# Attention and two MLPs on one core: where the second MLP's weight slabs and next inputs are requested, and an empty step in the weight preparation

## The chip, the cores and the metric

One core of one Trainium2 chip runs the whole program in one launch. The metric is the device time of that core in microseconds; the kernel before took 999.39 us (median of three runs, 997.2 to 1000.39).

## The reference, cut to what matters

```
attn  = softmax(causal(q k^T / 8 + min(-(cum_i - cum_j), 0))) v     B=4, H=8, S=576, D=64
x     = attn as 2304 tokens x 512
h     = x @ w_in1 (512x2048);  g = max(h,0) + alpha*min(h,0);  x = g @ w_out1 (2048x512)
h     = x @ w_in2 (512x2048);  g = max(h,0)^2;                  out = g @ w_out2 (2048x512)
```

All inputs are float32, and cum is the running sum of max(s, 0).

## The kernel before

Each float32 operand of a matmul is split into a high and a low part, and each product is three matmuls (high by high, high by low, low by high). TensorE (PE) therefore has three times the plain work, and the rest of the program is built around keeping it fed.

The program has three parts. **Attention** comes first. **The first MLP** walks 48 steps: three passes of 768 tokens (two halves of 384), and 16 blocks of 128 hidden units in each. One step has 24 matmuls of the first product (line 551, tiles ph) and 24 of the second (line 672, tiles po); VectorE (DVE) applies the activation to ph (lines 570, 571), ScalarE (ACT) and DVE split the result into gs (lines 573, 574), and both split the weights of the next step (lines 526, 527: wi_hi and wi_lo, wo_hi and wo_lo). At the change of a pass the finished sums are copied out of PSUM (evac, lines 260 and 262) and the next inputs are split (xs, lines 537 and 538).

**The second MLP** multiplies 2x2 blocks with seven products in place of eight (the Winograd form of Strassen's scheme), again in three passes. A pass has a first stage (stage1: eight blocks q, seven products of six matmuls in each, line 790, weights w1h) and a second (Stage2.run: 28 items of 18 matmuls, line 917, weights w2s and inputs th). The first stage's weights come from DRAM in groups (w1_group: tile w1f, four buffers, split by ACT and DVE into w1h, five buffers; four groups to a block q, 32 to a pass). The second stage's come in slabs of 1 MB (w2_slab: tile w2s, four buffers, 14 to a pass). The inputs of the next pass come with load_x (four requests, tile xl). All of these are requests on one queue, SyncE's (SP), which works in order.

These weights don't exist in the inputs: they are sums of blocks of w_in2 and w_out2, and the program makes them **during the first MLP**. A list todo says at which of the 48 steps each piece of that work is emitted. For w_in2 a block q is prep_conv twice (two ACT copies at lines 114 and 115, two DVE operations at 116 and 117, an addition on GpSimd (POOL) at 120, which together rebuild one weight tile from raw_w into the tile wc) and prep_sums (four POOL additions in wc and a store of wc to w1D, line 156). There is one buffer of wc, so the next block's first write into it, ACT's at line 115, has to wait until the store has read it. For w_out2 a block is two prep_conv, prep_sums and two prep_split (whl, lines 164 and 165, then a store to w2D). The pieces are spread evenly over steps 13 to 44 by their position in the list.

The order on each engine is not the order of the source. The compiler's planner reorders instructions by its own estimate of when each is ready, within what the data allow; a block `with tc.issue_after(x)` holds what it contains behind instruction x in that order. In the kernel before nothing holds the slabs and the next inputs of the second MLP, which is why they stand on SP's queue where the planner thought that they could go.

Words used below: a **group** is one w1f request with its split into w1h; a **slab** is one w2s request.

Of the kernel before, what the change touches and what calls it, by code (L numbers as in the profile page):

```python
# [19 lines left out]
def attention_then_two_mlps(  # L20
# [13 lines left out]
    nc = tc.nc  # L34
# [12 lines left out]
    NPASS = B * S // (2 * HT)  # L47
    NQ = NF // 2
# [84 lines left out]
    SLOT = {1: 0, 6: 1, 5: 2, 2: 3, 7: 4, 4: 5, 3: 6}  # L133
    w1D = dr.tile([NQ, P, 7, 256], F32, name="w1D")
# [423 lines left out]
    def ins_of(x):  # L558
        return x.ins if hasattr(x, "ins") else x
# [47 lines left out]
    for g in range(len(units) + LAG + PVLAG):  # L607
        live = g < len(units)
        if live:
            n, i = units[g]  # L610
            i = g % 5
# [75 lines left out]
    sub = []  # L687
    for which in range(2):
        for q_ in range(NQ):
            loads += [(1, q_ + z * NQ, which) for z in range(2)]  # L690
            sub += [(prep_conv, (which, q_, 0)), (prep_conv, (which, q_, 1)), (prep_sums, (which, q_))]
            if which:
                sub += [(prep_split, (q_, 0)), (prep_split, (q_, 1))]
    first_prep, last_prep = NF - NPRE, (NPASS - 1) * NF + NF - NPRE - 1
    todo += [(first_prep + (last_prep - first_prep) * z / len(sub), *t) for z, t in enumerate(sub)]
    for _ in range(2):
# [7 lines left out]
    def split2(dst, src):  # L704

        a = nc.scalar.copy(dst[:, 0], src)  # L706
        v = nc.vector.tensor_sub(dst[:, 1], src, dst[:, 0].bitcast(F32))  # L707
        return ins_of(a), ins_of(v)

    def load_x(p):  # L710
        xl = xa01.tile([P, NKB, W], F32, name="xl", tag="x0")
        for i, j in ((0, 0), (0, 1), (1, 1), (1, 0)):
            r, c = slice(2 * i, 2 * i + 2), slice(j * HT, (j + 1) * HT)
            nc.sync.dma_start(xl[:, r, c], xD[p][:, r, c])
        xl_now[0] = xl
# [5 lines left out]
    def x_steps():  # L721


        xl = xl_now[0]
        x_parts()
        b11, b12, b21, b22 = (xl[:, 2 * i : 2 * i + 2, j * HT : (j + 1) * HT] for i in range(2) for j in range(2))

        def put(i, src):
            split2(xc[i], src)

        def diff(dst, a, b):
            nc.vector.tensor_sub(dst, a, b)

        return [
            lambda: put(1, b11), lambda: diff(b12, b12, b11), lambda: put(5, b12),
            lambda: diff(b12, b22, b12), lambda: put(6, b12), lambda: diff(b11, b12, b11),
            lambda: put(2, b21), lambda: put(7, b11), lambda: diff(b21, b21, b12),
            lambda: put(4, b21), lambda: put(3, b22),
        ]

    GROUPS = ((0, 2), (2, 2), (4, 2), (6, 1))

    def w1_group(q, g):
        s0, k = GROUPS[g]
        wt = pools["w1"].tile([P, 512], F32, name="w1f", tag="w1f", bufs=4)
        nc.sync.dma_start(wt[:, : k * 256].rearrange("p (k c) -> p k c", k=k), w1D[q][:, s0 : s0 + k, :])
        hl = pools["w1"].tile([P, 2, 512], F32R, name="w1h", tag="w1h", bufs=5)
        split2(hl[:, :, : k * 256], wt[:, : k * 256])
        return hl

    def w2_slab(s, hq):
        t = pools["m2"].tile([P, 2, 4, 256], F32R, name="w2s", tag="w2s", bufs=4)
        nc.sync.dma_start(t.bitcast(F32), w2D[s, hq])
        return t
# [9 lines left out]
    class Stream:  # L764
# [5 lines left out]
        def fetch(self, n):  # L770
            while self.next < min(len(W1_ORDER), n):
                self.ready[W1_ORDER[self.next]] = w1_group(*W1_ORDER[self.next])
                self.next += 1
# [76 lines left out]
    class Stage2:  # L850


        def __init__(self, p):
            self.p = p
            self.items = [(i, q) for i in ORDER2 for q in range(NQ // 2)]
            self.th, self.slab, self.done = {}, {}, 0

        def prepare(self, n):

            while self.done < min(n, len(self.items)):  # L860
                i, q = self.items[self.done]
                self.done += 1
                if q % 2 == 0:
                    self.slab[i, q // 2] = w2_slab(SLOT[i], q // 2)
                gq = g_t[q]
                if i == 6:
                    nc.vector.tensor_sub(gq[:, :, 1], gq[:, :, 3], gq[:, :, 1])
                elif i == 7:
                    nc.vector.tensor_sub(gq[:, :, 0], gq[:, :, 1], gq[:, :, 0])
                elif i == 4:  # L870
                    nc.vector.tensor_sub(gq[:, :, 2], gq[:, :, 2], gq[:, :, 1])
                th = pools["m2"].tile([P, 2, 2, HT], F32R, name="th", tag="th", bufs=3)
                self.last = split2(th, gq[:, :, PLACE[i]])
                self.th[i, q] = th
# [130 lines left out]
    for p in range(NPASS):  # L1005
        s2 = Stage2(p)

        def early(left):
            if left == 0:
                s2.prepare(AHEAD)  # L1010
            if left == NQ // 2 and p + 1 < NPASS:
                load_x(p + 1)

        stage1(stream if p == 0 else Stream(), early)
        steps2 = x_steps() if p + 1 < NPASS else []

        def fill(n):
            if n >= 3 and n % 2 == 1 and steps2:
                with tc.issue_after(s2.last[0]), tc.issue_after(s2.last[1]):
                    steps2.pop(0)()  # L1020

        s2.run(fill)
        assert not steps2
# [30 lines left out]
```

## Time and profile before

| | us |
|---|---|
| median of three runs | 999.39 |
| lowest and highest run | 997.2, 1000.39 |
| profiled execution: span from first to last instruction | 998.7 |
| PE busy in it | 970.2 (97%) |
| DVE, ACT, POOL busy | 806.6 (81%), 561.9 (56%), 401.5 (40%) |
| granted TensorE clock, mean | 0.990 |

The page gives the profiled execution by its span alone, 998.7 us; it lies 0.7 us under the median of the runs. PE is the engine whose idle time counts; the busy share of the others says only how close they are to becoming the ones that PE waits for. The trace also gives the granted clock of each stretch: 1.00 is 2.4 GHz, 0.50 is 1.2 GHz, and values between are mixtures over the stretch.

### The profile page before, as it was taken

What the parts mean: (1) busy time and instruction counts of PE and PEld (TensorE: products, weight loads), DVE (VectorE), ACT (ScalarE), POOL (GpSimd) and SP (SyncE); (2) the same over time, 40 slices, a digit from 0 to 9 for tenths busy, and PEclk for the clock granted to TensorE, in tenths of its full rate; (3) what the DMA queues carried; (4) which work ended last, traced back from release to release, by engine and by line L of the source; (5) the groups of instructions that cost most, each with busy time, mean ns of one, the idle gap of its engine ahead of it and who ended that gap; (6) DMA issues with size and microseconds to landing.
All of it is one profiled execution on the core that took longest, in us unless ns stands there. A gap on an engine that the chain in (4) does not pass through costs nothing.

```text
span 998.7 us, 18060 instructions
## 1 busy us (share of the span) xinstructions
PE 970.2 (97%) x6440; PEld 899.7 (90%) x6440; DVE 806.6 (81%) x1552; ACT 561.9 (56%) x1120; POOL 401.5 (40%) x478
## 2 busy tenths in 40 slices
PE   6999999999999999999999999899999999999998
PEld 6677778788999989989999999899999999999998
DVE  8899889869888897878887768578985889668774
ACT  7788889964555544434554434456453664446442
POOL 7788777634333445553342220335002440034400
PEclk9899999999999999999999999989999999999999
DMA  7766454304444334436454341944687446754274
GB/s 175 172 155 162 121 123 119 73 19 142 127 127 127 133 126 159 158 127 201 150 170 134 127 142 40 365 128 148 219 274 268 127 155 236 266 179 130 97 250 139
DMA packets 105050, 157.06 MB, mean 157 GB/s; under 512 B 31584, under 2 KB 80224, under 8 KB 99584
## 3 DMA queue, kind: packets, MB, share of 16 engines
q1 hardware_dynamic: 104960, 155.91, 49.7%
q8 instruction: 51, 0.84, 0.3%
q14 instruction: 39, 0.32, 0.1%
HBM read 117.00 MB, written 29.88 MB: 147 GB/s over the span
## 4 chain that ended last, share of the span: by engine, by line
PE 68%; DVE 14%; DMA 6%; POOL 4%; ACT 4%; issue 4%; SPq 0%; DVEq 0%; POOLq 0%; ACTq 0%
PE acc L917 15%; PE ph L551 11%; PE po L672 10%; PE b L790 4%; PE a L790 4%; PE c L790 4%; PE ps_tr L443 3%; PE ps_xb L493 3%; PE d L790 2%; PE ps_xa L482 2%; DMA w1D<-wc 2%; PE ps_sc L357 2%; DVE gg L570 2%; PE ps_sc L358 2%; POOL wc L120 2%
## 5 line engine op out<-in xcount | busy, mean ns | idle before, releaser
L551 PE MATMUL ph<-xs,wi_hi 128*128 128x384 f32 x768 | 197.0, 336 | 3.4 <-DVE gg L571 2.6
L917 PE MATMUL acc<-w2s,th 128*128 128x256 f32 x1512 | 184.7, 283 | 3.2 <-ACT th L706 3.0
L917 PEld LDWEIGHTS acc<-w2s,th 128*128 128x128 f32 x1512 | 183.3, 192 | 4.2 <-ACT th L706 3.4
L672 PE MATMUL po<-gs,wo_hi 128*128 128x512 f32 (+1 forms) x768 | 167.5, 337 | 2.0 <-DVE xT L262 1.1
L551 PEld LDWEIGHTS ph<-xs,wi_hi 128*128 128x128 f32 x768 | 136.4, 188 | 7.2 <-DVE gg L571 3.8
L672 PEld LDWEIGHTS po<-gs,wo_hi 128*128 128x128 f32 x768 | 121.4, 189 | 16.5 <-DVE xT L262 1.3
L551 PE MATMUL ph<-xs,wi_lo 128*128 128x384 f32 x384 | 128.9, 336 | 0.0
L706 ACT CAST th<-g 128x768 fp32r<-128x768 f32 x84 | 69.8, 836 | 74.8 <-PE acc L917 57.2
L120 POOL TENSOR_TENSOR wc<-cv_t,wc 128x512 uint32<-128x512 uint32 x32 | 48.0, 1506 | 144.0 <-DVE cv_t L117 111.1
L707 DVE TENSOR_TENSOR th<-g,th 128x768 fp32r<-128x768 f32 x84 | 84.2, 1010 | 23.6 <-ACT th L706 23.5
L573 ACT CAST gs<-gg 128x768 fp32r<-128x768 f32 (+1 forms) x48 | 39.8, 829 | 106.1 <-DVE gg L571 106.1
L672 PE MATMUL po<-gs,wo_lo 128*128 128x256 f32 (+1 forms) x384 | 99.1, 336 | 0.0
L801 POOL TENSOR_TENSOR g<-g 128x384 f32<-128x384 f32 x24 | 21.8, 906 | 177.7 <-ACT g L800 120.5
L411 POOL TENSOR_SCALAR pr<-pr,rs 128x128 f32<-128x128 f32 (+3 forms) x128 | 74.0, 592 | 42.9 <-DVE rs L408 17.8
L707 DVE TENSOR_TENSOR w1h<-w1f,w1h 128x512 fp32r<-128x512 f32 (+1 forms) x96 | 68.9, 726 | 24.1 <-ACT w1h L706 23.2
L398 ACT ACTIVATE pr<-pr,nmax 128x128 f32<-128x128 f32 (+3 forms) x128 | 71.3, 559 | 16.9 <-DVE nmax L386 11.1
L706 ACT CAST w1h<-w1f 128x512 fp32r<-128x512 f32 (+1 forms) x96 | 53.7, 564 | 48.0 <-PE b L790 25.6
L574 DVE TENSOR_TENSOR gs<-gg,gs 128x768 fp32r<-128x768 f32 (+1 forms) x48 | 48.1, 1002 | 37.4 <-ACT gs L573 37.4
L120 POOL TENSOR_TENSOR wf<-cv_t,wf 128x512 uint32<-128x512 uint32 x32 | 45.8, 1431 | 74.0 <-DVE cv_t L117 71.9
L551 PEld LDWEIGHTS ph<-xs,wi_lo 128*128 128x128 f32 x384 | 72.4, 188 | 0.3 <-issue 0.2
L570 DVE TENSOR_SCALAR gg<-ph,alpha_sb 128x384 f32<-128x384 f32 x95 | 57.9, 609 | 13.8 <-PE ph L551 13.5
L801 POOL TENSOR_TENSOR g<-u 128x384 f32<-128x384 f32 x48 | 50.4, 1049 | 41.5 <-ACT u L800 41.2
(157 smaller groups left out, 2131.4 us busy)
## 6 DMA issues: line engine op xcount, KB each, us to landing
w2s<-w2D SPq DMA_DIRECT2D x42, 1024.0 KB
w1f<-w1D SPq DMA_DIRECT2D x72, 256.0 KB
raw_w<-in_moe_w_in_dram SPq DMA_DIRECT2D x32, 512.0 KB
w2D<-whl SPq DMA_DIRECT2D x16, 896.0 KB
raw_w<-in_moe_w_out_dram SPq DMA_DIRECT2D x24, 512.0 KB
w1D<-wc SPq DMA_DIRECT2D x8, 896.0 KB
QM<-QS SPq DMA_DIRECT2D x15, 288.0 KB
KH<-KS SPq DMA_DIRECT2D x15, 288.0 KB
```

Of the source, the lines that this page charges most:

```text
L120: nc.gpsimd.tensor_tensor(d, t, d, ALU.add)
L398: last = nc.scalar.activation(o, o, AF.Exp, bias=m, scale=-1.0, accum_out=sums[:, h : h + 1])
L411: nc.gpsimd.tensor_scalar(pr[:, :w], pr[:, :w], rs[:, h : h + 1], 1.0, ALU.mult, ALU.mult)
L551: nc.tensor.matmul(ph[h][:, :HT], ws[a][:, kb * P : (kb + 1) * P], xs[kb][:, bb, h * HT : (h + 1) * HT], start=(cnt == 0), stop=(cnt == 3 ...
L570: nc.vector.tensor_scalar(x, ph[h][:, :HT], 0.0, alpha_sb[:, f : f + 1], ALU.min, ALU.mult)
L574: sub = nc.vector.tensor_sub(z[:, 1], a, z[:, 0].bitcast(F32))
L672: nc.tensor.matmul(acc, ws[a][:, m * P : (m + 1) * P], gs[:, bb, c_], start=first_ and z == 0, stop=lst and z == 2, skip_group_check=True,)
L706: a = nc.scalar.copy(dst[:, 0], src)
L707: v = nc.vector.tensor_sub(dst[:, 1], src, dst[:, 0].bitcast(F32))
L790: nc.tensor.matmul(pt[:, :HT], hl[:, a, c0 + kb * P : c0 + (kb + 1) * P], xc[i][:, b, kb, :], start=(first and cnt == 0), stop=(cnt == 5), ...
L801: nc.gpsimd.tensor_tensor(dst, r, r, ALU.mult)
L917: nc.tensor.matmul(acc[tb // 2][:, (tb % 2) * 256 : (tb % 2 + 1) * 256], th[:, x, qq, tb * P : (tb + 1) * P], ws[:, y, (2 * q + qq) % 4, : ...
```

## The change

Two edits. First, the list of preparation pieces gets one more entry behind each prep_sums of w_in2: a function that does nothing. The list is 72 long in place of 64, so that every piece's step moves. Second, every group's request is remembered in last_w1. Behind each block q of the first stage the function early now runs inside `issue_after(last_w1[0])`: at q = 3 it requests the next pass's inputs, and at q = 4, 5, 6 and 7 it requests one of the first four slabs each; prepare no longer requests a slab that is already there. Before, early requested the inputs at the same place in the source but held by nothing, and the slabs were requested by prepare, the first one behind block 7.

```diff
@@ -691,6 +691,8 @@
             if which:
                 sub += [(prep_split, (q_, 0)), (prep_split, (q_, 1))]
+            else:
+                sub += [(lambda: None, ())]
     first_prep, last_prep = NF - NPRE, (NPASS - 1) * NF + NF - NPRE - 1
     todo += [(first_prep + (last_prep - first_prep) * z / len(sub), *t) for z, t in enumerate(sub)]
@@ -738,12 +740,14 @@
+    last_w1 = [None]
     def w1_group(q, g):
         s0, k = GROUPS[g]
         wt = pools["w1"].tile([P, 512], F32, name="w1f", tag="w1f", bufs=4)
-        nc.sync.dma_start(wt[:, : k * 256].rearrange("p (k c) -> p k c", k=k), w1D[q][:, s0 : s0 + k, :])
+        d = nc.sync.dma_start(wt[:, : k * 256].rearrange("p (k c) -> p k c", k=k), w1D[q][:, s0 : s0 + k, :])
+        last_w1[0] = ins_of(d)
@@ -855,13 +859,16 @@
+        def fetch(self, i, hq):
+            self.slab[i, hq] = w2_slab(SLOT[i], hq)
         def prepare(self, n):
             while self.done < min(n, len(self.items)):
...
-                if q % 2 == 0:
-                    self.slab[i, q // 2] = w2_slab(SLOT[i], q // 2)
+                if q % 2 == 0 and (i, q // 2) not in self.slab:
+                    self.fetch(i, q // 2)
@@ -1006,10 +1013,14 @@
         def early(left):
+            with tc.issue_after(last_w1[0]):
+                if left < 4:
+                    i, q = s2.items[2 * (3 - left)]
+                    s2.fetch(i, q // 2)
+                if left == NQ // 2 and p + 1 < NPASS:
+                    load_x(p + 1)
             if left == 0:
                 s2.prepare(AHEAD)
-            if left == NQ // 2 and p + 1 < NPASS:
-                load_x(p + 1)
```

**Place 1, SP's queue where the second MLP begins.** xD is the store of the first MLP's last sums, xl the next inputs, w1f a group, w2s a slab. Before:

```order
L680 DMA xD_90<-xT_85 128x768
L714 DMA xl<-xD_89 128x2x384 x2
L746 DMA w1f<-w1D 128x512
L753 DMA w2s<-w2D 128x2048 x4
L746 DMA w1f<-w1D 128x512 x2
L746 DMA w1f<-w1D 128x256
L746 DMA w1f<-w1D 128x512 x3
```

Now:

```order
L680 DMA xD_90<-xT_85 128x768 x3
L749 DMA w1f<-w1D 128x512 x3
L749 DMA w1f<-w1D 128x256
L749 DMA w1f<-w1D 128x512 x3
L749 DMA w1f<-w1D 128x256
L716 DMA xl<-xD_89 128x2x384 x4
L749 DMA w1f<-w1D 128x512 x3
L749 DMA w1f<-w1D 128x256
L757 DMA w2s<-w2D 128x2048
L749 DMA w1f<-w1D 128x512 x3
L749 DMA w1f<-w1D 128x256
L757 DMA w2s<-w2D 128x2048
```

The inputs stood ahead of the tenth group and the four slabs right behind it. Now the inputs stand behind the 17th group, and the slabs behind the 21st, 25th, 29th and 32nd.

**Place 2, ACT at the end of w_in2's preparation** (wc the write that waits for the store, gs the split of the activation, wi_hi the next step's weights). Before:

```order
L114 ACTIVATE cv_g<-raw_w 128x512 x2
L526 CAST wo_hi<-wf 128x512
L115 ACTIVATE wc<-raw_w 128x2x256 x2
L526 CAST wi_hi<-wf 128x512
L573 CAST gs<-gg 128x768
L114 ACTIVATE cv_g<-raw_w 128x512
L526 CAST wo_hi<-wf 128x512
L115 ACTIVATE wc<-raw_w 128x512
L526 CAST wi_hi<-wf 128x512
L573 CAST gs<-gg 128x768
```

Now:

```order
L526 CAST wo_hi<-wf 128x512
L526 CAST wi_hi<-wf 128x512
L573 CAST gs<-gg 128x768
L114 ACTIVATE cv_g<-raw_w 128x512
L115 ACTIVATE wc<-raw_w 128x2x256
L114 ACTIVATE cv_g<-raw_w 128x512
L115 ACTIVATE wc<-raw_w 128x2x256
L526 CAST wo_hi<-wf 128x512
L526 CAST wi_hi<-wf 128x512
L573 CAST gs<-gg 128x768
L114 ACTIVATE cv_g<-raw_w 128x512
L526 CAST wo_hi<-wf 128x512
```

The last row before the next wc is the same in both; a step without any conversion (its first three rows here) now stands ahead of the block's pair of writes.

**Place 3, DVE where pass 0 goes from its first stage to its second** (th the split inputs of an item, g, xl and xc the differences and splits that also have to be made there). Before:

```order
L707 TENSOR_TENSOR th<-g,th 128x768
L732 TENSOR_TENSOR xl<-xl 128x2x384
L869 TENSOR_TENSOR g<-g 128x2x384
L825 TENSOR_TENSOR g<-g 128x2x384
L867 TENSOR_TENSOR g<-g 128x2x384
L869 TENSOR_TENSOR g<-g 128x2x384
L707 TENSOR_TENSOR th<-g,th 128x768 x2
```

Now:

```order
L709 TENSOR_TENSOR th<-g,th 128x768
L829 TENSOR_TENSOR g<-g 128x2x384
L876 TENSOR_TENSOR g<-g 128x2x384
L874 TENSOR_TENSOR g<-g 128x2x384
L709 TENSOR_TENSOR th<-g,th 128x768
L734 TENSOR_TENSOR xl<-xl 128x2x384
L709 TENSOR_TENSOR th<-g,th 128x768
```

Five operations stood between one th and the next; now at most three do. In passes 1 and 2 PE, DVE, ACT and POOL keep the order that they had, and only SP's requests move.

## Rows read from the trace of the kernel before

**Rows 1.** The page's first part: busy time and share of the span by engine.
```profile
PE 970.2 (97%) x6440; PEld 899.7 (90%) x6440; DVE 806.6 (81%) x1552; ACT 561.9 (56%) x1120; POOL 401.5 (40%) x478
```
**Rows 2.** Waits of PE, whole span: us in total, times, longest.
```profile
PE acc L917 <- ACT th L706: 3.0, 2, 1.5
PE d L790 <- ACT w1h L706: 3.0, 1, 3.0
PE ph L551 <- DVE gg L571: 2.6, 2, 2.2
PE po L672 <- DVE xT L262: 1.1, 1, 1.1
...
PE ph L551 <- DVE xs L538: 0.6, 1, 0.6
```
**Rows 3.** Stretches: length, busy (instructions) of PE, PEld, DVE, ACT, POOL; clock, DMA share, GB/s.
```profile
646.00:649.16 3.16, 0.17 (x1) 0.00 (x1) 1.93 (x4) 1.16 (x3) 1.75 (x3) 0.89 0.79 290
649.16:656.23 7.07, 7.07 (x25) 7.07 (x25) 4.52 (x9) 3.27 (x7) 0.00 (x0) 0.57 0.55 170
628.00:648.00 20.00, 18.16 (x105) 17.84 (x103) 10.29 (x17) 9.29 (x18) 7.48 (x9) 1.00 1.02 397
439.00:443.80 4.80, 4.80 (x18) 4.54 (x19) 3.90 (x7) 3.08 (x5) 1.77 (x3) 0.64 0.42 134
756.00:808.00 52.00, 52.00 (x302) 52.00 (x301) 39.53 (x66) 31.79 (x64) 23.52 (x25) 1.00 0.51 158
```
**Rows 4.** Timeline of SP's queue, second MLP's start: start, length, request, count.
```profile
631.84 0.52 SPq L746 DMA_DIRECT2D w1f<-w1D  x1
632.45 1.97 SPq L753 DMA_DIRECT2D w2s<-w2D  x4
635.14 57.46 SPq L746 DMA_DIRECT2D w1f<-w1D  x29
```
**Rows 5.** Timeline of ACT, 648 to 653 us: idle before and its releaser in brackets.
```profile
648.49 2.26 ACT L706 CAST w1h<-w1f 128x512 fp32r<-128x512 f32 x4 [1.18 <-DMA w1f<-w1D]
652.51 0.62 ACT L706 CAST w1h<-w1f 128x512 fp32r<-128x512 f32 x1 [1.76 <-DMA w1f<-w1D]
```
**Rows 6.** Tile w1f, 649.5 to 653.4 us, SP alone: ns min/median/max, first and last start.
```profile
L746 SPq DMA_DIRECT2D w1f<-w1D x4: 319/320/378, 649.9 to 651.5; - x4
```
**Rows 7.** Tile w1f in pass 1, 796.5 to 801.7 us.
```profile
L746 SPq DMA_DIRECT2D w1f<-w1D x4: 319/319/320, 796.7 to 801.2; - x4
L706 ACT CAST w1h<-w1f x4: 407/616/624, 797.2 to 801.6; 128x512 fp32r<-128x512 f32 x3, 128x256 fp32r<-128x256 f32 x1
```
**Rows 8.** Waits of ACT, 756 to 816 us (first stage of pass 1): the longest.
```profile
ACT w1h L706 <- PE b L790: 10.6, 7, 6.7
```
**Rows 9.** Timeline of PE, 428 to 446 us.
```profile
438.99 0.62 PE L551 MATMUL ph<-xs,wi_hi 128*128 128x384 f32 x2 [2.23 <-DVE gg L571]
```
**Rows 10.** Timelines of POOL, SP, ACT and DVE around that wait.
```profile
423.73 3.00 POOL L120 TENSOR_TENSOR wc<-cv_t,wc 128x512 uint32<-128x512 uint32 x2 [4.42 <-DVE gg L571]
...
431.00 0.33 SPq L156 DMA_DIRECT2D w1D<-wc  x1
...
422.98 1.23 ACT L115 ACTIVATE wc<-raw_w 128x512 uint32<-128x512 uint32 x2 [2.76 <-DMA w1D<-wc]
...
435.92 0.66 ACT L115 ACTIVATE wc<-raw_w 128x512 uint32<-128x512 uint32 x1 [7.77 <-DMA w1D<-wc]
...
437.12 1.35 DVE L527 TENSOR_TENSOR wi_lo<-wf,wi_hi 128x512 fp32r<-128x512 f32 x1 [3.95 <-ACT wi_hi L526]
438.39 0.55 DVE L571 SCALAR_TENSOR_TENSOR gg<-ph,gg 128x384 f32<-128x384 f32 x1
```
**Rows 11.** Waits of ACT, 220 to 470 us.
```profile
ACT wc L115 <- DMA w1D<-wc: 30.9, 8, 7.8
```
**Rows 12.** Timeline of PE: the second stage's first matmuls in pass 0; a wait in pass 1.
```profile
688.47 1.35 PE L917 MATMUL acc<-w2s,th 128*128 128x256 f32 x10
...
829.21 1.71 PE L917 MATMUL acc<-w2s,th 128*128 128x256 f32 x12 [1.52 <-ACT th L706]
```

## The prediction

> **What bounds the kernel now.** I read the page's busy times first: PE works through 970.2 of 998.7 us [rows 1]. No other engine comes near, so the kernel's time is PE's work plus what PE loses (some 28 us). The second view is the list of PE's waits, which says what the loss in the two MLPs consists of [rows 2]: 3.0 us once in the second MLP for the weights w1h, 3.0 us in two waits of 1.5 for th, 2.6 us in two waits for gg in the first MLP (one of 2.2), 1.1 us where the MLPs meet, 0.6 us for xs. The third view is the table of stretches, which shows what this list hides: behind the 3.0 us PE is busy and yet slow, since its granted clock over the next 7.07 us is 0.57, that is mostly the lower level (1.2 GHz) after 1.00 before the wait [rows 3]. Behind the wait of 2.2 us the same is seen, 0.64 over 4.8 us. So each of the two long waits is paid nearly twice, and the change is aimed at both.
>
> **Part 1, the requests in the second MLP.** Why does PE wait 3.0 us? SP's queue answers [rows 4]: one group at 631.84, then four slabs from 632.45, and only then the next 29 groups. From 628 to 648 us all DMA engines are full (share 1.02, 397 GB/s [rows 3]); ACT, which has to split the groups, stands until 648.49 for a group's landing and then splits four at once [rows 5]. The groups that PE needed were queued behind 4 MB of slabs that nobody reads before 688.47 [rows 12], and behind the next inputs. With the order now, groups alone stand in this place, and a slab follows each fourth group later on.
>
> What it gives: the idle 3.00 us. And the clock: 7.07 us hold 24 matmul starts [rows 3] (25 less the one cut at the edge); at full clock one takes 52/300 = 0.173 us (pass 1's first stage, which runs 52 us without a gap, 302 less two edges), so 24 take 4.16 and 2.91 us come back. Together **5.9 us**. Lower bound: nothing, if the next groups come late for a new reason (below); upper bound: this sum, there is no more loss in that stage.
>
> What it costs: each slab now passes ahead of later groups, in all three passes, and so do the inputs (1.5 MB) in passes 0 and 1. A slab takes 1.05 MB/397 GB/s = 2.6 us, the inputs 4.0. A group landed 2.6 us after its request when little stood ahead (request at 649.9 [rows 6], ACT's split at 652.51 [rows 5]). In pass 1 a request is made 4.9 us before its split: four groups are in flight, the one requested at 796.7 is split at 801.6 [rows 7], and these splits wait for PE to hand back a w1h buffer (10.6 us in seven waits), not for a landing [rows 8]. Behind a slab a group lands after 2.6 + 2.6 = 5.2 us, 0.3 late; behind the inputs after 6.6, 1.7 late. Five w1h buffers mean that four earlier groups are still to be used when a group is split, at 1.8 us each (a block of 7.3 us has four groups), so some 7 us lie between the split and its use. I take **0 us**; the bound on the other side is rival 3. The slabs themselves are asked for behind blocks 4 to 7, at 42 x 0.173 = 7.3 us a block; the last is needed when the seventh item begins, so they are not late. SP issues four more times nothing: the same requests, in another order.
>
> A rule of the Trainium skill speaks against this part ("DMA: Bandwidth & Descriptors", section "Rules for kernel authors": issue a DMA early, wait late). By it the old order is the better one and part 1 would bring nothing (995.1 in place of 989.2, about what rival 2 gives). The rows above show the price of early in a queue that serves in order, so I go by them.
>
> **Part 2, the empty step.** The second long wait [rows 9] goes back over four engines [rows 10]: PE needs ph, freed by DVE's gg (438.39); that stood behind wi_lo (437.12), which waited for ACT's wi_hi; and ACT stood 7.77 us at its write into wc until 435.92, because the store requested at 431.00 was still reading wc. ACT stood there once for every block, eight times, 30.9 us [rows 11], and only the longest reached PE: 7.77 less 2.23 leaves 5.5 us that the order can swallow.
>
> Why so long? One block is a chain: ACT's write (422.98), POOL's additions from 423.73 to the store at 431.00, the store's end at 435.92: 12.9 us from write to write. A step is 48 x 0.173 = 8.3 us. The list gave a block three entries of 31/64 step, 12.1 us: less than the chain, so that each block ran later than planned and the debt grew. Now it gives four entries of 31/72 step, 14.3 us: more than the chain. Pieces go out at whole steps: the first writes fall on steps 15, 17, 19, 20, 22, 24, 26 and 27. Two steps (16.6 us) leave no wait; the two single ones (19 to 20, 26 to 27) leave 12.9 - 8.3 = 4.6 us, under the 5.5. So the wait on PE should go: 2.23 idle, and 0.36 x 4.8 = 1.7 of clock [rows 3], **3.9 us**. Bounds: 0 if a single step still overruns, 3.9. The wait for xs (0.6 [rows 2]) comes behind two conversions in one step at the first change of pass; now there is one, so ACT starts the xs splits 0.6 us earlier: **0.6 us**, bound 0.
>
> What it costs: w_out2's preparation gets 31 x 40/72 = 17.2 steps in place of 19.4, the same work in 11% less time, and at the second change of pass (steps 31 to 33) two conversions and four whl splits where there were two and two. DVE is the tightest there. The trace shows no wait of this kind in that place; bounds are nothing and one more stall like that of rows 9 with its clock, 3.9 us. I take **1.0 us** lost, nearer to nothing, since no wait in that part of the first MLP reaches PE today.
>
> **Part 3, side effects of the reordering.** Of the two waits for th, the one in pass 1, at 829.21 [rows 12], stays: nothing is reordered there on the engines. For the one in pass 0 five DVE operations between two th have become three at most, but DVE has the same work: between 0 and 1.5 us gained, I take **0.75**. The 1.1 us where the MLPs meet stay.
>
> **Sum.** 998.7 - 5.9 - 3.9 - 0.6 - 0.75 + 1.0 = 988.5 us of span. The median of the runs stands 0.7 above this profiled execution, so I forecast **989.2 us**. About 0.3% (3 us) is what a measurement of this kernel can tell from no change.
>
> **Rivals.**
> 1. Part 2 does not deliver: the wait in the first MLP stays or moves to the second change of pass. For it: only 0.9 us lie between 4.6 and 5.5, and the w_out2 part gets denser. Against: seven waits out of eight are swallowed today. Then 999.4 - 5.9 = 993.5.
> 2. Part 1 does not deliver: pass 0's first stage waits for something else, for instance the planner's new order of products there. Then 999.4 - 3.9 - 0.6 = 994.9. Against: pass 1's first stage does the same work for 52 us without a gap [rows 3].
> 3. Slower: groups come late behind the inputs and slabs. Place: block 4 of each pass and the next. It decides if the landing is later than the 4.9 us of lead plus the 7 us of w1h buffers. Price: a stall like the present one, 5.9 us, in each pass: pass 0 keeps what it has, passes 1 and 2 get one each, and part 2 gives about 4, so 999.4 + 11.8 - 4 = 1007. Against: 5.2 and 6.6 us against 11.9. The Trainium skill ("DMA: Bandwidth & Descriptors", section "Bandwidth") gives 6.15 us for a lone megabyte; by that figure a group behind a slab would land after 8.8 us (estimate), still inside, but with ACT held up 3.9 us each time. The 20 us at 397 GB/s decide for 2.6.
> 4. Nothing happens, because other waits take over both places: 999.4.
>
> **How the numbers follow.** The forecast 0.60 (986 to 992: all gains without the 1.0 give 987.5, with th's full 0.75 more 986.7; a loss of 3.9 in place of 1.0 gives 992), rival 1 0.17, rival 2 0.09, rival 3 0.06, rival 4 0.08. The range 985 to 995.5 takes in the forecast's own range with the scatter of the runs (997.2 to 1000.4) and rivals 1 and 2, and leaves out 3 and 4. Faster by over 0.3% (below 996.4): 0.60 + 0.17 + 0.09 = 0.86, same 0.08, slower 0.06.
>
> **What would show it.** Right: no PE wait for w1h in the second MLP and a clock of 1.00 through 620 to 660 us; SP's timeline with slabs singly between groups; DMA share well under 1 there; ACT's total wait for w1D at a third of 30.9 or less; no PE wait for gg over 1 us. Wrong: a stall of 2 us or more at steps 31 to 33 or behind block 3 of a pass, each with a fall of the clock behind it.

## The result, and the profile after

The changed kernel took 990.89 us (median of six runs, 988.28 to 992.2), the kernel before on the same chip 1000.83 (six runs, 997.2 to 1002.96): ratio 0.9907, 95% interval 0.9891 to 0.9923. The forecast of 989.2 us lies 1.7 us below the median and inside the runs. Its sum is less good than its total, as the parts below show. The profiled execution of the changed kernel has a span of 989.0 us.

The busy times, beside [rows 1]:

```profile
PE 965.1 (98%) x6440; PEld 895.8 (91%) x6440; DVE 806.6 (82%) x1552; ACT 561.7 (57%) x1120; POOL 393.3 (40%) x478
```

PE is 5.1 us less busy with the same 6440 matmuls: time at the lower clock, 4.7 us of it, had counted as busy. The list of PE's waits, beside [rows 2] (us in total, times, longest):

```profile
PE acc L924 <- ACT th L708: 2.0, 2, 1.8
PE acc L924 <- DVE th L709: 1.1, 1, 1.1
PE po L672 <- DVE xT L262: 1.1, 1, 1.1
...
PE b L794 <- DVE u L816: 0.6, 1, 0.6
```

The waits for w1h, for xs and for gg are gone. Waits for th (the split inputs of a second-stage item) are still 3.1 us in all, and a wait for u (a partial result of the first stage, made by DVE) is new.

**Where part 1 aimed.** SP's queue at the second MLP's start, beside [rows 4], and the stretches there, beside [rows 3]; the last of these is the second change of pass in the first MLP:

```profile
626.50 15.22 SPq L749 DMA_DIRECT2D w1f<-w1D  x8
641.76 1.96 SPq L716 DMA_DIRECT2D xl<-xD  x4
643.83 4.33 SPq L749 DMA_DIRECT2D w1f<-w1D  x4
648.25 0.38 SPq L757 DMA_DIRECT2D w2s<-w2D  x1
651.24 5.09 SPq L749 DMA_DIRECT2D w1f<-w1D  x4
656.38 0.42 SPq L757 DMA_DIRECT2D w2s<-w2D  x1
```

```profile
628.00:648.00 20.00, 20.00 (x117) 20.00 (x117) 16.55 (x26) 11.95 (x24) 8.33 (x9) 1.00 0.52 167
649.00:656.00 7.00, 7.00 (x42) 7.00 (x41) 5.94 (x9) 5.34 (x11) 5.46 (x6) 1.00 0.84 306
460.00:520.00 60.00, 60.00 (x347) 56.47 (x346) 52.62 (x79) 31.81 (x50) 19.72 (x18) 1.00 0.62 202
```

The slabs stand singly between the groups, the DMA share from 628 to 648 us is 0.52 in place of 1.02, PE has no gap and its clock is 1.00.

**Where part 2 aimed.** ACT's waits from 220 to 470 us, beside [rows 11]:

```profile
ACT wc L115 <- DMA w1D<-wc: 14.2, 6, 4.3
```

Less than half of 30.9 us, the longest 4.3 in place of 7.8: under the 5.5 us that the order can swallow. The prediction's sign for this was a third or less (10.3 us); that sign is missed. The step at 480 to 520 us, for which the prediction set 1.0 us aside, has no gap (the last stretch above).

**What the prediction did not have.** PE where pass 1 goes from its first stage to its second (idle time before, in brackets), beside the single wait of 1.52 in [rows 12]:

```profile
801.57 1.32 PE L794 MATMUL b<-xc,w1h 128*128 128x384 f32 x6 [0.61 <-DVE u L816]
...
816.03 1.70 PE L924 MATMUL acc<-w2s,th 128*128 128x256 f32 x12 [1.08 <-DVE th L709]
819.56 2.67 PE L924 MATMUL acc<-w2s,th 128*128 128x256 f32 x17 [1.82 <-ACT th L708]
```

3.51 us are lost here in place of 1.52. Read backwards: ACT's waits in the first stage of pass 1 (in the kernel before ACT waits there for no landing of w1f), then two rows of DVE's timeline, then SP's queue ahead of them, and last the first use of pass 2's weights.

```profile
ACT w1h L708 <- DMA w1f<-w1D: 7.3, 5, 2.6
```

```profile
798.20 0.62 ACT L708 CAST w1h<-w1f 128x512 fp32r<-128x512 f32 x1 [2.62 <-DMA w1f<-w1D]
```

```profile
794.94 0.41 DVE L709 TENSOR_TENSOR w1h<-w1f,w1h 128x256 fp32r<-128x256 f32 x1
...
798.85 0.69 DVE L709 TENSOR_TENSOR w1h<-w1f,w1h 128x512 fp32r<-128x512 f32 x1 [2.45 <-ACT w1h L708]
```

```profile
789.80 0.42 SPq L757 DMA_DIRECT2D w2s<-w2D  x1
790.57 13.29 SPq L749 DMA_DIRECT2D w1f<-w1D  x7
```

```profile
866.42 1.22 PE L794 MATMUL b<-xc,w1h 128*128 128x384 f32 x6
```

The group requested at 790.57 is split at 798.20, 7.6 us later and directly behind a landing. The slab 0.8 us ahead of it is the fourth of the pass, which stands behind the 32nd and last group: so the late group is the first one of pass 2 (the 256 wide split at 794.94 is the last of pass 1), and PE has no use for it before 866.42. DVE, which keeps its order, stood 2.45 us for that split all the same, and from then on it is busy almost without a break until 821 us (21.5 of 22.2 us): u for the wait at 801.57 and th for the other two are made late. So the reading is that slabs between groups cost 2.0 us in pass 1. It had to be tested, since the same stretch lost 1.52 us before anyway.

**How executions are compared below.** The first wait of PE in the first MLP (po for gs, 0.9 us) is the same in every profile, but it comes at times from 229.3 to 233.9 us in the twelve executions of this study, though no edit touches the part of the program before it. This scatter of attention, 4.6 us, is as large as the effects in question. Single profiles are therefore compared from that wait to the end of the span (called the **rest**), and only timed runs by ratio.

### The profile page after: what moved, and what is told of

Its sections match the earlier page's. It is cut to its first block, busy times and chain, and to the rows that moved or that the text cites. A ratio compares the mean times of both kernels' runs of the same rounds, so it can differ in the third digit from the quotient of the medians.

```text
span 989.0 us, 18064 instructions
## 1 busy us (share of the span) xinstructions
PE 965.1 (98%) x6440; PEld 895.8 (91%) x6440; DVE 806.6 (82%) x1552; ACT 561.7 (57%) x1120; POOL 393.3 (40%) x478
## 4 chain that ended last, share of the span: by engine, by line
PE 77%; DVE 11%; DMA 4%; ACT 3%; issue 3%; POOL 1%; SPq 0%; DVEq 0%; ACTq 0%; POOLq 0%
PE acc L924 17%; PE ph L551 16%; PE po L672 15%; PE b L794 4%; PE a L794 4%; PE c L794 4%; PE ps_tr L443 3%; PE ps_xb L493 3%; PE ps_xa L482 2%; PE d L794 2%; DMA KH<-KS 2%; PE ps_sc L357 2%; PE ps_sc L358 2%; DMA w1f<-w1D 1%; PE ps_sc L363 1%
## 5 line engine op out<-in xcount | busy, mean ns | idle before, releaser
L709 DVE TENSOR_TENSOR th<-g,th 128x768 fp32r<-128x768 f32 x84 | 81.7, 979 | 22.4 <-ACT th L708 22.3
L709 DVE TENSOR_TENSOR w1h<-w1f,w1h 128x512 fp32r<-128x512 f32 (+1 forms) x96 | 73.8, 776 | 22.7 <-ACT w1h L708 22.1
L526 ACT CAST wi_hi<-wf 128x512 fp32r<-128x512 f32 x48 | 29.8, 621 | 71.4 <-PE ph L551 69.7
```

## The experiments

**The parts by themselves.** The kernel before with the empty step alone:

```diff
             if which:
                 sub += [(prep_split, (q_, 0)), (prep_split, (q_, 1))]
+            else:
+                sub += [(lambda: None, ())]
```

> The kernel before with the empty step alone. If part 2 is worth its idle time and its clock together and stands by itself, the 2.2 us wait for gg, 1.7 us of clock and the small waits for xs and gg (1.0 us) go: 4.9 us, ratio to before 0.995; the wait of 3.0 us for w1h and the slow 7 us behind it stay. Rival: the clock's share is not gained but only moved, then idle alone: 3.2 us, ratio 0.9968. Rival: the preparation that is now denser costs something at the second change of pass that the changed kernel hides: ratio 0.996 to 1.0, with a wait between 480 and 520 us.

Measured: 995.51 us against 1001.2, ratio 0.9943 (0.9922 to 0.9965). No wait for gg or xs is left. The wait for w1h is there, but look at the clock behind it:

```profile
643.24 0.61 PE L792 MATMUL d<-xc,w1h 128*128 128x384 f32 x2 [2.92 <-ACT w1h L708]
```

```profile
643.30:650.00 6.70, 6.70 (x39) 6.67 (x40) 4.78 (x10) 3.80 (x8) 0.09 (x1) 1.00 0.55 168
```

2.92 us of idle time and 1.00 afterwards, where [rows 3] had 0.57. Part 2 stands by itself; that a wait of this length is paid a second time does not hold in each execution. The profiled execution is the fastest of the seven, with a mean clock of 0.998 over the whole program; the other six have 0.990 to 0.993, so one profile does not say how often the clock falls behind this wait.

The changed kernel without the empty step:

```diff
             if which:
                 sub += [(prep_split, (q_, 0)), (prep_split, (q_, 1))]
-            else:
-                sub += [(lambda: None, ())]
```

> The changed kernel without the empty step. If the second MLP's gains are additive: 5.9 us (wait and clock) and 1.4 us of the th wait in pass 0 are gained, 2.0 us are lost at the change of stage in pass 1: 5.3 us, ratio 0.9947, with the first MLP's wait of 2.2 us for gg as before. Rival: idle time alone counts (3.0 + 1.4 - 2.0): 2.4 us, ratio 0.9976. Rival: the parts need each other, ratio 1.0.

Measured: 996.72 us, ratio 0.9963 (0.9947 to 0.9979), between the first two cases. The parts add up: 3.7 us here and 5.7 with the empty step alone, together 9.4, where the change as a whole gave 9.3. That they need each other is ruled out. The wait for w1h is gone, the waits at the change of stage in pass 1 are there as in the changed kernel (0.80, 1.09, 1.83). And the clock again does something else than in the first profile: behind a wait of 2.36 us for gg it stays up, behind the waits of pass 1 it falls.

```profile
442.01 0.61 PE L551 MATMUL ph<-xs,wi_hi 128*128 128x384 f32 x2 [2.36 <-DVE gg L571]
```

```profile
442.00:447.00 5.00, 4.99 (x28) 4.66 (x29) 4.07 (x7) 2.99 (x5) 1.97 (x3) 1.00 0.44 139
...
825.80:831.00 5.20, 5.13 (x30) 5.13 (x31) 5.20 (x6) 2.65 (x5) 0.00 (x0) 0.67 0.02 5
```

**Is the clock's fall a property of the wait?** The kernel before was profiled twice more, with no edit.

> The kernel before once more, for one profile. Theory: a wait of PE lets the granted clock fall in some executions and not in others: the waits of 2.2 us (gg) and 3.0 us (w1h) are there within 0.2 us, but behind at least one of them the clock stays at 1.00 in this or in the next run. Rival: the clock falls behind both each time, as in the first profile (0.64 over 4.8 us, 0.57 over 7 us), and it was the change of the code that kept it up in the runs of one part alone.

> The kernel before a third time, for another profile: theory and rival as for the run ahead of it (waits of 2.2 and 3.0 us there again; the clock at 1.00 behind at least one of the four, or below 0.7 behind all).

Measured (998.97 and 997.74 us, spans 997.2 and 996.0): the first three rows are the one execution, the others the next.

```profile
439.97 0.62 PE L551 MATMUL ph<-xs,wi_hi 128*128 128x384 f32 x2 [2.17 <-DVE gg L571]
```

```profile
440.00:444.80 4.80, 4.80 (x19) 4.65 (x20) 3.91 (x7) 3.06 (x5) 1.77 (x3) 0.64 0.40 139
650.50:657.50 7.00, 7.00 (x40) 7.00 (x41) 5.29 (x10) 4.06 (x9) 0.59 (x1) 1.00 0.57 170
```

```profile
440.51 0.62 PE L551 MATMUL ph<-xs,wi_hi 128*128 128x384 f32 x2 [2.13 <-DVE gg L571]
```

```profile
440.50:445.30 4.80, 4.79 (x27) 4.50 (x28) 3.88 (x7) 3.00 (x5) 1.77 (x3) 1.00 0.41 148
649.20:656.20 7.00, 6.98 (x40) 6.98 (x41) 5.29 (x10) 4.07 (x9) 0.56 (x1) 1.00 0.54 170
```

The waits repeat within 0.1 us for gg and 0.3 us for w1h (3.29 and 3.08). The clock does not: of these four it fell behind one. The three executions of the kernel before lost 4.7, 1.7 and 0 us to the lower clock behind the first MLP's start (sum over stretches of 2 us of their length times what the clock lacks to 1.00), 2.1 in the mean.

**Does the empty step act by the spacing of the blocks?** The eight empty entries were put behind all of w_in2's entries, so that the list is as long but a block has three entries:

```diff
-            else:
-                sub += [(lambda: None, ())]
+    sub[NQ * 3:NQ * 3] = [(lambda: None, ())] * NQ
     first_prep, last_prep = NF - NPRE, (NPASS - 1) * NF + NF - NPRE - 1
```

> The changed kernel with the eight empty entries moved to the end of w_in2's part of the list: the list is 72 long as before, but a block has three entries, 31/72 x 3 x 8.3 = 10.7 us. If the spacing of the blocks is what the empty step gives (a chain of 12.9 us from write to write), the debt grows faster than in the kernel before: ACT waits for wc longer than the 30.9 us of before, the longest over 7.8, and the wait of PE for gg is back, 2.2 us or more; ratio to before 0.994 or more. Rival: the gain comes from any stretching or other position of the list (the last block's neighbours alone): no PE wait for gg, ratio 0.9907 as for the changed kernel.

Measured: 995.59 us against 1000.33, ratio 0.9951 (0.9933 to 0.9969). The wait of PE for gg is back, at another step, though ACT's wait for wc did not grow (over 30.9 us was expected, it is 13.9):

```profile
399.52 0.69 PE L551 MATMUL ph<-xs,wi_hi 128*128 128x384 f32 x1 [2.19 <-DVE gg L571]
```

```profile
ACT cv_g L114 <- DMA raw_w<-in_moe_w_in_dram: 14.6, 8, 5.4
ACT wc L115 <- DMA w1D<-wc: 13.9, 5, 4.4
```

```profile
396.08 0.66 ACT L114 ACTIVATE cv_g<-raw_w 128x512 f32<-128x512 f32 x1 [5.37 <-DMA raw_w<-in_moe_w_in_dram]
396.65 0.61 ACT L526 CAST wi_hi<-wf 128x512 fp32r<-128x512 f32 x1
```

The eight stores go out from 343.58 to 431.73 us, 12.6 us apart in the mean, as in the kernel before (341.11 to 431.00, 12.8 apart): the blocks run at the pace of their chain, with 10.7 us in the list and with 12.1. In the changed kernel, whose list gives 14.3, they go out from 342.28 to 442.09, 14.3 apart: there the list sets the pace. What the list gives less than the chain takes has to be waited for, and the planner put that wait at the landing of raw_w, 5.37 us, with wi_hi and so gg behind it. So the spacing decides; the place of the wait, which I had expected at wc, does not.

**Which requests make the loss in pass 1?** Two kernels that differ from the changed one on SP's queue alone; PE, DVE, ACT and POOL have the same instructions in the same order. In the first the new requests are in pass 0 only:

```diff
-            with tc.issue_after(last_w1[0]):
+            if p == 0:
+                with tc.issue_after(last_w1[0]):
...
+            if p > 0 and left == NQ // 2 and p + 1 < NPASS:
+                load_x(p + 1)
```

> The changed kernel with the new requests in pass 0 alone; on PE, DVE, ACT and POOL every instruction stands where it stood, only SP's order in passes 1 and 2 goes back to that of before. Theory: slabs between the groups make these land late in pass 1, DVE falls behind and PE loses some 3.5 us at the change of stage in place of 1.5: here the loss falls back to about 1.5 us, ACT no longer waits for w1f in pass 1, the ratio to before is 0.9887 (2 us under the changed kernel's 0.9907). Rival: DVE is behind there by itself, whatever the requests: the loss stays at 3.5 us and the ratio at 0.9907. Rival: four slabs at the head of the queue cost a wait for w1h in pass 1, too, as in pass 0 of the kernel before: a PE wait for w1h, ratio 0.993 or more.

In the second the inputs stay held in pass 1, too, and only the slabs of passes 1 and 2 go back:

```diff
-                if left < 4:
+                if p == 0 and left < 4:
```

> As the run with the new requests in pass 0 alone, but the next inputs stay behind block 3 in pass 1 too; only the slabs of passes 1 and 2 go back to the head of the queue. If the slabs make the groups late, this run equals that one: 0.9887, loss at the change of stage 1.5 us, at most one wait of ACT for w1f in pass 1 (1.0 us, behind the inputs). If the inputs do it: loss 3.5 us and 0.9907, as in the changed kernel.

Measured: 989.58 us, ratio 0.9889 (0.9865 to 0.9913), and 989.15 us, ratio 0.9885 (0.986 to 0.991), against 1001.2. Both lose 1.52 us at the change of stage in pass 1, as the kernel before. The second one's waits, PE from 640 us on and ACT for groups in pass 1:

```profile
PE acc L924 <- ACT th L708: 1.7, 2, 1.5
```

```profile
ACT w1h L708 <- DMA w1f<-w1D: 1.3, 1, 1.3
```

The slabs do it; the inputs cost ACT one wait of 1.3 us that does not reach PE. From the changed kernel to these two the rest falls by 3.1 and 2.7 us (758.5 to 755.4 and 755.8), of which 2.0 are the waits named. The intervals of both ratios overlap that of the changed kernel (0.9891 to 0.9923), so the gain over it is shown by the traces.

**Which requests made the wait in pass 0?** One half of the new requests each, in all passes: first the slabs held and the inputs as early as before, then the other way round.

```diff
             with tc.issue_after(last_w1[0]):
                 if left < 4:
                     i, q = s2.items[2 * (3 - left)]
                     s2.fetch(i, q // 2)
-                if left == NQ // 2 and p + 1 < NPASS:
-                    load_x(p + 1)
             if left == 0:
                 s2.prepare(AHEAD)
+            if left == NQ // 2 and p + 1 < NPASS:
+                load_x(p + 1)
```

> The changed kernel with the slabs held behind the groups, but the next inputs requested as early as before (in pass 0 at the head of the queue, 1.6 MB, in pass 1 between the stores). If it is the amount of data ahead of the groups that made the wait for w1h (3.0 us with 4 slabs and the inputs, 5.8 MB), 1.6 MB take 4 us at 397 GB/s and the wait is gone or under 0.5 us; pass 1 loses at its change of stage as the changed kernel does (about 3.5 us), since the slabs do that. Ratio 0.9907. Rival: the inputs alone make it: a wait of PE for w1h of 2 us or more in pass 0.

```diff
             with tc.issue_after(last_w1[0]):
-                if left < 4:
-                    i, q = s2.items[2 * (3 - left)]
-                    s2.fetch(i, q // 2)
                 if left == NQ // 2 and p + 1 < NPASS:
                     load_x(p + 1)
```

> The changed kernel with the next inputs held behind block 3, but the slabs requested where the planner puts them (in pass 0 four at the head of the queue, 4.2 MB). If the slabs made the wait, it is back: PE waits for w1h about 1.5 to 3 us in pass 0 (10.6 us of transfers at 397 GB/s in place of 14.6), and pass 1 loses no more than 1.6 us at its change of stage; ratio about 0.991 to 0.993, with or without a fall of the clock behind the wait. Rival: the inputs made it: no wait for w1h, ratio 0.9889.

Measured: 989.88 us, ratio 0.9898 (0.9877 to 0.992), and 989.4 us, ratio 0.9887 (0.986 to 0.9914), against 999.49. With 1.6 MB of inputs at the head of the queue PE waits for no w1h; with 4.2 MB of slabs there it waits 1.9 us in three waits:

```profile
PE d L794 <- ACT w1h L708: 1.1, 2, 0.8
PE c L794 <- ACT w1h L708: 0.8, 1, 0.8
```

The waits grow with the amount ahead of the groups, as expected: 5.8 MB for 3.0 us, 4.2 for 1.9, 1.6 for none. Whether slabs count by anything but their size was not tried. The second run's ratio is not the expected one (0.991 to 0.993) but the rival's (0.9889, no wait for w1h); the trace, which has the wait, decides against the rival, and that pass 1 lost less than was allowed for is part of the difference. At the change of stage in pass 1 the first of the two loses 0.93 and 1.83 us, the second 0.21: the slabs again. In the first one ACT waits in pass 1 for two landings only, and 2.62 of the 2.8 us are for the first group of pass 2, as in the changed kernel: so the loss for th goes with this late group and not with those behind the earlier slabs. These two kernels also reorder the engines a little, so their times are not compared to a tenth.

**The rest of the loss in pass 1.** What is left in pass 1, the 1.52 us, was put down to DVE: an xc split and an xl difference stand between its th splits. To the kernel with the new requests in pass 0 alone one edit was added, which moves these steps behind item 7 in passes 1 and 2 (only pass 1 has such steps):

```diff
-            if n >= 3 and n % 2 == 1 and steps2:
+            if n >= (7 if p else 3) and n % 2 == 1 and steps2:
```

> The run with the new requests in pass 0 alone, and in pass 1 the eleven steps that split the next inputs begin behind item 7 in place of item 3. Theory: what is left of the loss at the change of stage in pass 1 is DVE's work (an xc split and an xl difference stand between the th splits, 1.8 us): the wait for th of 1.52 us goes below 0.3, ratio to before 0.9874 (1.5 us under that run's 0.9889). Rival: the work that is moved makes a later th late, or the first product of pass 2 waits for xc: no gain, 0.989 or more.

Measured: 987.07 us against 1000.33, ratio 0.988 (0.9863 to 0.9898). PE passes the change of stage without a stop:

```profile
804.97 1.22 PE L794 MATMUL c<-xc,w1h 128*128 128x384 f32 x6
806.02 24.19 PE L924 MATMUL acc<-w2s,th 128*128 128x256 f32 x197
```

Behind attention PE's waits of 0.2 us and more are down to one of 1.07 (where the MLPs meet) and one of 0.21, and the rest to 753.6 us. The interval of this ratio overlaps that of the run without the edit (0.9889); that the 1.5 us are gained is shown by the trace, not by the ratio.

## Why the prediction was right, and where not

Seven of the profiles, from the first wait of the first MLP to the end, in us. Idle is the sum of PE's waits of 0.2 us or more behind that wait, clock the loss to the lower level; what remains is the work.

| execution | rest | idle | clock | remains |
|---|---|---|---|---|
| before, first profile | 769.3 | 10.3 | 4.7 | 754.3 |
| before, third profile | 764.8 | 10.3 | 0 | 754.5 |
| empty step alone | 760.5 | 7.0 | 0 | 753.5 |
| requests alone | 765.0 | 9.3 | 1.7 | 754.0 |
| the change | 758.5 | 4.8 | 0 | 753.7 |
| requests in pass 0 alone | 755.4 | 2.8 | 0 | 752.6 |
| that, and xc later in pass 1 | 753.6 | 1.3 | 0 | 752.3 |

Idle time and clock explain the differences up to some 2 us. What is left goes along with the order of the rows (small waits under 0.2 us would do it, but this was not tried).

**Part 1, gain 5.9 us.** The cause was right: the four slabs and the inputs in front of the groups, and the more of them the longer the wait. The 3.00 us of idle time are gained. The 2.91 us of clock were the step that failed: "each of the two long waits is paid nearly twice" was read from one execution, and behind this wait the clock fell in one of four profiles that have it (three of the kernel before, one with the empty step alone). Alone the new requests gave 3.7 us (interval 2.1 to 5.3), where parts 1 and 3 were put at 6.65.

**Part 1, cost 0 us.** This is the second step that failed. The lateness was foreseen for groups behind inputs (1.7 us) and slabs (0.3 us), but priced by w1h's buffers, which did hold: PE never waits for w1h, and the late group that did the harm was not due for another 68 us. What gave way was DVE, which works in order and has no time to spare at the change of stage in pass 1. And the size was off: a group behind a slab landed after 7.6 us, not 5.2. The estimate of 8.8 us in rival 3, which the prediction set aside, was nearer. 397 GB/s was the rate of a full queue of bulk transfers; around this slab, 789.8 to 798.2 us, it was lower:

```profile
789.80:798.20 8.40, 8.40 (x53) 8.40 (x52) 5.63 (x11) 3.18 (x8) 4.04 (x5) 1.00 0.83 284
```

The cost was 2.0 us, all in pass 1; pass 0 and pass 2 show none. It is rival 3's cause at another place: groups late behind a slab, but at the change of stage and in one pass, not at block 4 of each, and for a third of its price per pass.

The rule of the Trainium skill that the prediction set aside ("DMA: Bandwidth & Descriptors", section "Rules for kernel authors": issue early, wait late) was wrong for the slabs of pass 0 and right for those of pass 1. In pass 0 early meant ahead of groups that were needed at once: 1.9 us of waits with the slabs there. In pass 1 early meant between the stores of the pass before, when no group was due, and going back to it gained 2.0 us.

**Part 2, gain 3.9 and 0.6 us, cost 1.0.** The chain against the spacing was right, and so was the longest wait for wc, 4.3 us (4.6 forecast); both waits for gg went, as did the one for xs: 3.2 us of idle time. How the waits are spread was not: the prediction has two single steps with 4.6 each and none at the double steps, the trace six waits with 14.2 in all, so pieces do not keep to whole steps as reckoned. The 1.7 us of clock come in some executions only (two of the three of the kernel before). The cost at the second change of pass did not come. Alone the step gave 5.7 us (0.9943; interval 3.5 to 7.8), against the 3.2 of idle time and 1.1 of clock in the mean of three profiles; the difference is inside the interval. Net the prediction had put part 2 at 3.5.

**Part 3.** The th wait in pass 0 shrank from 1.52 to 0.21 us, 1.3 in place of 0.75.

**The sum** came out by some luck, because the errors are opposite: the requests gave less than forecast and the empty step more. Idle time was forecast to fall by 5.6 us (3.00 + 2.23 + 0.6 + 0.75 - 1.0) and fell by 5.5: the 2.0 us lost in pass 1 are made up by the 1.0 that did not come, 0.6 more for th and the second, small wait for gg (0.4), which was not counted. The clock was forecast to give 4.6 us; in the mean of three executions of the kernel before it can give 2.1. The timed runs agree: the mean clock of the whole program is 0.9926 over the 40 timed runs of the kernel before that have it on record, and 0.9947 over the six of the changed kernel, an estimated 2.1 us of 1000 (attention's clock is in both). Some 0.6 us of work remain between the two kernels in the table. Together 8.2 us, where 10.2 were forecast (999.4 to 989.2) and 9.3 measured, interval 7.7 to 10.9. Two of the prediction's bounds, 987.5 and 986.7, are spans; as medians they are 0.7 higher.

## What to carry to other kernels

Where a queue serves in order, count the bytes that stand ahead of the next piece that is due: bulk goes ahead when nothing is due, and behind it otherwise; the same four slabs were harmful early in one pass and harmless early in the next. When a transfer is made later on purpose, follow its lateness through every engine that works in order to the place with the least slack, since that place (DVE at a change of stage here) pays, and not the buffer in front of PE. That holds for a piece that nobody needs yet, too: here one that was due 68 us later held up DVE; a version that makes it later on DVE as well was not tried. Before a fall of the clock is entered in a sum, look at it in several executions.

## What the runs showed of the hardware that I had not expected

- The granted clock behind one and the same wait differs between executions of one program. Behind 2.1 to 2.4 us (for gg) it fell three times, to 0.64, 0.64 and 0.66, and stayed at 1.00 twice; behind 2.9 to 3.3 us (for w1h) it fell once in four. Behind the waits at the change of stage in pass 1 (the longest 1.8 us) it fell in two of four executions. Behind a single wait of 1.5 us, of which the profiles have ten, it never fell. The Trainium skill ("TensorE: Matmul & The Clock Gate", section "Part 1: The HAM clock gate") says that the gate's looking does not start with the kernel, which would make it a matter of chance whether a wait counts; no run here tried that.
- The end of attention, whose code no edit touches, lies up to 4.6 us apart in twelve executions (1.8 us in the three of the kernel before), more than most steps of this study.
- A group of 256 KB behind a slab of 1 MB needed 7.6 us from request to split, though the DMA engines were not full (share 0.83).
